# Fewer weight tiles decoded beside attention, a reordered drain and one PSUM layout in a fused attention and feed-forward kernel

## Chip, core and metric

One core of a Trainium2 chip runs the whole program in one launch. The metric is the device time of one execution in microseconds: 1037.8 us before the change, median of 3 runs (1034.76 to 1038.8).

## What is computed

Three stages follow each other. Attention, over 4 batches, 8 heads, 576 positions, 64 columns a head:

```python
scores = scale * np.matmul(q, k.transpose(0, 1, 3, 2))       # causal mask, softmax -> a
local = np.matmul(a, v)
mem_out = einsum(phi(q), M_prev) / (einsum(phi(q), z_prev) + 1e-06)
x = g * mem_out + (1 - g) * local                            # 2304 tokens x 512
```

A first feed-forward stage with weights of 512 x 2048 and 2048 x 512, and a second of two 512 x 1024, one 1024 x 1024 and one 1024 x 512:

```python
h = x @ w_in;  x = (h * np.tanh(softplus(h))) @ w_out
a = x @ w1;  b = x @ w2;  out = ((a * b) @ w3) @ w_out2
```

The weights of the two feed-forward stages come as 64-bit floating-point numbers, and the kernel turns them into 32-bit numbers itself.

## The kernel before, in words

**Decoding weights.** A tile of weights (128 x 512, 64-bit) is loaded as pairs of words into a buffer `draw`; six DVE instructions (L114 to L127) and one POOL addition (L132) turn it into 32-bit numbers `da`; two more POOL instructions split the result into a rounded part and a remainder (L77 and L80, or L160 and L161 where the result goes back to DRAM). `decode` (L104) emits this for a list of tiles, step by step over the list; `run` (L135) takes the next n jobs of a generator. `decoder` (L98) sets up the buffers: one raw buffer and one `da` beside attention, three raw and two `da` in the first feed-forward stage.

**Attention.** There are 16 pairs of heads, p = 0 to 15, in the loop at L521, which also runs once more (p = 16) to finish the last pair. For a pair: scores into `psA` (`s_blocks` L381, `s_last` L397), maximum by DVE (L374), exponential by ACT (L379), normalisation by DVE and POOL (`normed` L358), transposes of the result through `psF` and copies by ACT (`pt_g` L422), and the product with v and the memory matrix in `psX` and `psF` (`pv` L433). `in_turn` (L69) runs a function so that its PE instructions stand behind the PE instruction traced last; before the change that holds from the first transpose on, in the drain at p = 16 too. The compiler's scheduler arranges everything else by a list in which earlier text has priority.

Beside the pairs the kernel decodes weights: at p = 2 to 11 one job each (L559) of a chain of two generators. The first, `lq0`, has the eight tiles of the first quarter of the first feed-forward stage, four of w_in and four of w_out. The second, `pre` (`predecode` L180), has sixteen tiles of the second stage's weights that are decoded early and put back into DRAM.

**First feed-forward stage.** It runs over 4 quarters g of the 2048 hidden columns and 6 chunks n of 384 tokens: 24 units (g, n). `emit_h` (L459) computes h of a unit into four PSUM banks, 48 matmuls of 384 columns, then tanh, arctan and sine by ACT and the product with h by DVE (L493). `split_y` (L496) splits the result y, and `emit_x2` (L593) multiplies it by w_out, again 48 matmuls, and adds into x2 in SBUF (L608, L610). PE runs h of a unit, then x2 of the unit before. Meanwhile the next quarter's eight tiles and the jobs of `pre` are decoded (L691 to L697). In the last quarter w3 and w_out2 are multiplied together (`fold` L615), between h and x2 of each unit.

h and y of unit (0, 0) are made at p = 16, after `pt_g` of group 5 (L553).

**Second feed-forward stage.** `emit_ab` (L739) makes two products a and b for 512 tokens and 128 columns at a time, and `emit_out` (L758) multiplies their product by the folded weights; five of these steps are between the two.

**PSUM before.** Eight banks. In attention: `psA`, two tiles of two banks; X and F, two banks each. After attention that pool is closed and another is opened with three banks A, three X and two F (L578 to L580). h takes A, A, F, F (in the last quarter A, A, A, X; in unit (0, 1) F, X, F, X), x2 takes X, a and b take A, A or A, F in turn, the output of a chunk X, X, X, F.

Of the kernel before, what the change touches and what calls it, by code (L numbers as in the profile page):

```python
# [21 lines left out]
def fused_kernel(ctx: ExitStack, tc, q, k, v, M_prev, z_prev, beta, w_in, w_out, w1, w2, w3, w_out2, out):  # L22
# [19 lines left out]
    sk = ExitStack()  # L42
    pool = [sk.enter_context(tc.tile_pool(name="ps0", bufs=1, space=PSUM))]
    banks = {"X": 2, "F": 2}

    def bank(tag):
        return pool[0].tile([128, 512], F32, tag=tag, name="ps" + tag, bufs=banks[tag])

    def psA():
        return pool[0].tile([128, 2, 512], F32, tag="A", name="psA", bufs=2)  # L50
# [10 lines left out]
    tail = [None]  # L61

# [6 lines left out]
    def in_turn(fn, *args):  # L69

        if tail[0] is None:
            return fn(*args)
        with tc.issue_after(tail[0]):
            return fn(*args)
# [23 lines left out]
    def decoder(stack, raw, n, w=WN):  # L98
        dec.update(pool=stack.enter_context(tc.tile_pool(name="dec", bufs=1)), raw=raw, n=n, w=w)
# [355 lines left out]
    HT = ("AAFF", "AAAX")  # L455
    HU = {(0, 1): "FXFX"}
    gt = {}

    def emit_h(u, beside=iter(())):  # L459
# [7 lines left out]
        for m in range(KQ):  # L467
            if u == (0, 0):
                if m % 2 == 0:
                    two = psA()  # L470
                o = two[:, m % 2, 0:CH]
            else:
                o = bank(HU.get(u, HT[g == NQ - 1])[m])[:, 0:CH]
            ms = slice(128 * m, 128 * m + 128)
            for kk in range(KD):
                mm(o, t[:, 0, kk, ms], x[:, 0, kk, cs], kk == 0, False)
                mm(o, t[:, 0, kk, ms], x[:, 1, kk, cs], False, False)
                mm(o, t[:, 1, kk, ms], x[:, 0, kk, cs], False, kk == KD - 1)
            hp.append(o)
            if m == 1:  # L480
                steps(beside, 1)
# [38 lines left out]
    background = chain(lq0, pre)  # L520
    for p in range(NPAIR + 1):  # L521

        now, old, new = p < NPAIR, p > 0, p + 1 < NPAIR
        if old:
            ensure_x((p - 1) // (2 * NP))
        if not now:
            ek.close()
            wps[0] = wk.enter_context(tc.tile_pool(name="wp", bufs=1, side="right"))
        if p + 2 < NPAIR:
            load_pair(p + 2)  # L530
            load_v(p + 2)
        if now:
            in_turn(s_blocks, p, (3,))
        if old:
            in_turn(pt_g, p - 1, 4)
            in_turn(pt_g, p - 1, 2)
# [11 lines left out]
        if not now:  # L548
            run(lq0, 100)
        if old:  # L550
            in_turn(pt_g, p - 1, 5)
            if not now:
                split = split_y((0, 0), emit_h((0, 0)))  # L553
            in_turn(pt_g, p - 1, 6)
# [4 lines left out]
        if 2 <= p < 12:  # L559
            run(background, 1)  # L560
# [4 lines left out]
        if old:  # L565
            in_turn(pv, p - 1)
        if now:
            in_turn(pt_g, p, 1)
# [6 lines left out]
        if now:  # L575
            normed(p, [(4, None)])
    at.close()
    sk.close()  # L578
    pool[0] = ctx.enter_context(tc.tile_pool(name="ps", bufs=1, space=PSUM))
    banks.update(A=3, X=3)  # L580
# [12 lines left out]
    def emit_x2(u, beside):  # L593
# [4 lines left out]
        for m in range(KD):  # L598
            o = psX()[:, 0:CH]
# [77 lines left out]
    for u in [(g, n) for g in range(NQ) for n in range(NCH)]:  # L677
        g, n = u
        last = g == NQ - 1
        if u not in gt:  # L680
# [4 lines left out]
            y = emit_h(u, folding if last and n > 0 else iter(()))  # L685
# [5 lines left out]
        with tc.issue_after(split):  # L691
            if u == (0, 0):
                run(pre, 2)
            if n == 0:
                run(pre, 2)
            elif not last:
                run(nextq if n < 4 else chain(islice(nextq, 1), islice(pre, 1)), 2)  # L697
        if last and n == 0:
# [41 lines left out]
    def emit_ab(k):  # L740
# [3 lines left out]
        pb, pa = (bank(t)[:, 0:n] for t in ("AA", "AF")[m % 2])  # L744
# [13 lines left out]
    def emit_out(k):  # L758
# [4 lines left out]
        if m == 0:  # L763
            outs[c] = [bank(tag) for tag in "XXXF"[0:n // 128]]
# [63 lines left out]
```

## Time and profile before

| | us |
|---|---|
| median of 3 runs | 1037.8 |
| profiled execution | 1035.9 |
| its span (first to last instruction) | 1034.1 |
| PE busy | 979.9 (95%) |
| DVE busy | 602.9 (58%) |
| ACT busy | 506.9 (49%) |
| POOL busy | 336.2 (33%) |

The profiled execution is a single one; its time is that of the span and what lies around it. Matmuls are pipelined, so a busy PE need not be PE at its fastest. Attention with its drain takes about the first 290 us, the first feed-forward stage runs to about 730 us, and the second to the end.

### The profile page before, as it was taken

The page shows a single profiled execution, that of the slowest core. Times are in us where ns is not written, and L with a number is a line of the kernel's source. Part 1 is how long each engine was busy: PE and PEld are TensorE (multiplying, and loading weights), DVE is VectorE, ACT ScalarE, POOL GpSimd, SP SyncE. Part 2 cuts the span into 40 slices and gives each one's busy share as a digit, 9 for nine tenths or more (in the row PEclk, how much of TensorE's full clock was granted, in tenths as well). Part 3 has the DMA queues.
Part 4 walks back from the last instruction along what each step waited for, and adds up shares of the span by engine and source line. Part 5 has one row for each costly group of instructions (what it writes and reads, how often), then busy time and mean ns, then how long its engine had stood idle before and what let it go on. Part 6 is the DMA issues. An engine that isn't in the chain of part 4 may idle for free.

```text
span 1034.1 us, 15144 instructions
## 1 busy us (share of the span) xinstructions
PE 979.9 (95%) x5584; PEld 830.1 (80%) x5584; DVE 602.9 (58%) x1364; ACT 506.9 (49%) x1016; POOL 336.2 (33%) x345
## 2 busy tenths in 40 slices
PE   5888888999899999999999999999989999999998
PEld 3445455565699999999999999999768888888897
DVE  4888988675377666757575676668973121121111
ACT  4676767888646565565656545443323121221212
POOL 6676666552155334352524221112550000000000
PEclk8998999999999999999999999999999999999999
DMA  7343434320143133112312356222410010100101
GB/s 157 93 114 93 96 93 122 91 52 14 61 143 102 46 117 106 59 61 103 123 41 82 137 193 226 91 78 82 152 41 1 1 41 1 41 1 1 41 1 61
DMA packets 93626, 81.73 MB, mean 79 GB/s; under 512 B 68720, under 2 KB 72816, under 8 KB 93552
## 3 DMA queue, kind: packets, MB, share of 16 engines
q1 hardware_dynamic: 92224, 80.44, 25.2%
q8 instruction: 44, 0.72, 0.3%
q10 hardware_dynamic: 1328, 0.33, 0.2%
q14 instruction: 30, 0.25, 0.1%
HBM read 65.54 MB, written 15.20 MB: 78 GB/s over the span
## 4 chain that ended last, share of the span: by engine, by line
PE 73%; DVE 13%; ACT 7%; POOL 2%; issue 2%; DMA 2%; SPq 0%; ACTq 0%; DVEq 0%; POOLq 0%
PE psX L64 30%; PE psA L64 24%; PE psF L64 17%; ACT s L379 3%; DVE s L374 2%; DVE s L369 2%; PE psF L67 1%; DVE da L118 1%; DVE phie L333 1%; ACT pt L431 1%; POOL s L369 1%; DVE da L114 1%; DVE xt L80 1%; DVE draw L127 1%; PE psF L634 1%
## 5 line engine op out<-in xcount | busy, mean ns | idle before, releaser
L132 POOL TENSOR_TENSOR da<-da,draw 128x512 f32<-128x512 f32 x72 | 104.8, 1464 | 333.6 <-DVE draw L127 253.3
L64 PE MATMUL psX<-gh,wqt 128*128 128x384 f32 x768 | 196.1, 335 | 0.0
L64 PEld LDWEIGHTS psX<-gh,wqt 128*128 128x128 f32 x768 | 138.8, 188 | 1.0 <-DVE y L493 0.3
L64 PE MATMUL psX<-gl,wqt 128*128 128x384 f32 x384 | 128.2, 335 | 0.0
L64 PE MATMUL psA<-xt,wqt 128*128 128x384 f32 x648 | 118.9, 335 | 0.0
L64 PEld LDWEIGHTS psA<-xt,wqt 128*128 128x128 f32 x648 | 112.8, 188 | 0.7 <-DVE s L369 0.2
L379 ACT ACTIVATE s<-s,acc 128x512 f32<-128x512 f32 (+2 forms) x144 | 83.7, 587 | 19.1 <-DVE acc L374 18.4
L67 PEld LDWEIGHTS psF<-ident,s 128*128 128x128 f32 x400 | 44.7, 144 | 55.2 <-ACT pt L431 13.3
L67 PE MATMUL psF<-ident,s 128*128 128x128 f32 x400 | 67.1, 294 | 19.8 <-DVE xt L80 8.0
L64 PE MATMUL psA<-x2h,w12t 128*128 128x512 f32 (+1 forms) x288 | 80.7, 355 | 4.2 <-POOL w12t L77 3.6
L64 PE MATMUL psX<-wft,room 128*128 128x512 f32 x336 | 82.6, 390 | 0.0
L431 ACT COPY pt<-psF 128x512 f32<-128x512 f32 (+1 forms) x112 | 56.9, 538 | 44.8 <-PE psF L67 42.2
L64 PE MATMUL psF<-xt,wqt 128*128 128x384 f32 x408 | 75.2, 339 | 2.8 <-DVE xt L80 2.8
L753 ACT COPY bs<-psA 128x512 f32<-128x512 f32 (+1 forms) x40 | 21.8, 545 | 114.2 <-PE psA L64 106.2
L64 PEld LDWEIGHTS psF<-xt,wqt 128*128 128x128 f32 x408 | 72.4, 191 | 2.9 <-DVE xt L80 2.9
L64 PEld LDWEIGHTS psX<-wft,room 128*128 128x128 f32 x336 | 62.6, 188 | 12.7
L64 PEld LDWEIGHTS psX<-gl,wqt 128*128 128x128 f32 x384 | 72.1, 188 | 0.3
L610 DVE TENSOR_TENSOR x<-x,psX 128x384 f32<-128x384 f32 x72 | 39.6, 549 | 53.7 <-PE psX L64 53.5
L374 DVE CUSTOM_DVE_ANT_0 s<-psA,mask 128x512 f32<-128x512 f32 (+2 forms) x144 | 62.7, 477 | 9.2 <-PE psA L64 9.2
L64 PE MATMUL psA<-x2s,w12t 128*128 128x512 f32 x288 | 67.9, 389 | 0.0
L501 ACT CAST gh<-y 128x768 fp32r<-128x768 f32 x48 | 40.1, 837 | 55.5 <-PE psX L64 53.4
L755 ACT CAST room<-bs 128x512 fp32r<-128x512 f32 (+1 forms) x40 | 23.1, 578 | 84.9 <-DVE bs L754 84.7
(123 smaller groups left out, 1896.2 us busy)
## 6 DMA issues: line engine op xcount, KB each, us to landing
draw<-in_moe_w_dram SPq DMA_DIRECT2D x32, 512.0 KB, 3.7
draw<-in_moe_w_out_dram SPq DMA_DIRECT2D x24, 512.0 KB, 3.8
draw<-in_moe_w_in_dram SPq DMA_DIRECT2D x16, 512.0 KB, 4.0
out_dram<-ob SPq DMA_DIRECT2D x18, 256.0 KB, 2.0
raw<-in_q_dram SPq DMA_DIRECT2D x32, 128.0 KB, 3.2
raw<-in_v_dram SPq DMA_DIRECT2D x32, 128.0 KB, 2.7
o_dram<-draw SPq DMA_DIRECT2D x8, 512.0 KB, 2.8
w_dram<-draw SPq DMA_DIRECT2D x8, 512.0 KB, 2.8
```

The source lines that it names most:

```text
L64: tail[0] = nc.tensor.matmul(o, lhsT=l, rhs=r, start=start, stop=stop).ins
L67: tail[0] = nc.tensor.transpose(o, src, ident).ins
L80: return (eng or nc.vector).tensor_tensor(out=dst, in0=src, in1=f(hi), op=ALU.subtract)
L132: nc.gpsimd.tensor_tensor(out=a, in0=a, in1=lw.bitcast(F32), op=ALU.add)
L369: (nc.gpsimd if x in ON_POOL else nc.vector).tensor_scalar(out=s, in0=s, scalar1=d["sum"][:, x:x + 1], scalar2=og[:, x:x + 1], op0=ALU.mul ...
L374: nc.vector.tensor_tensor_reduce(out=s, in0=o, in1=m, op0=ALU.add, op1=ALU.min, scale=-scale, scalar=init, accum_out=a,)
L379: nc.scalar.activation(out=s, in_=s, func=AF.Exp, scale=-1.0, bias=a, accum_out=r)
L431: nc.scalar.copy(out=t[:, 0:n], in_=o[:, 0:n])
L501: nc.scalar.copy(out=gh, in_=y[i])
L610: r = nc.vector.tensor_tensor(out=d, in0=d, in1=o, op=ALU.add)
L753: nc.scalar.copy(out=bs, in_=pb)
L755: nc.scalar.copy(out=t[:, 0, 0:n], in_=bs)
```

## The change

- Beside the pairs only four jobs of `lq0` are decoded, w_in's four tiles, at p = 3, 6, 9 and 12. w_out's four are decoded at p = 16, two at a time, with a decoder of its own (two raw buffers, two `da`) in the space that attention's early pool has given back.
- The tiles of `pre` come later: none beside pairs, two in unit (0, 0) instead of four, one more each in (1, 0), (1, 2), (2, 0) and (2, 2).
- At p = 16, h of (0, 0) with its y stands first, before the transposes of the last pair; h of (0, 1) follows `pv` of the last pair.
- `in_turn` orders PE only for pairs 1 to 15, and not in pair 0 and the drain.
- PSUM keeps one layout throughout: two `psA` tiles of two banks, two banks X, two F. h takes the two `psA` tiles; x2 takes X and F in turn in quarters 0 to 2 and X alone in the last; a and b take the halves of one `psA` tile; the output of a chunk takes X, F, X, F.

```diff
-    banks = {"X": 2, "F": 2}
+    ps = ctx.enter_context(tc.tile_pool(name="ps", bufs=1, space=PSUM))
...
     def in_turn(fn, *args):
 
-        if tail[0] is None:
+        if not ordered[0]:
             return fn(*args)
...
         for m in range(KQ):
-            if u == (0, 0):
-                if m % 2 == 0:
-                    two = psA()
-                o = two[:, m % 2, 0:CH]
-            else:
-                o = bank(HU.get(u, HT[g == NQ - 1])[m])[:, 0:CH]
+            if m % 2 == 0:
+                two = psA()
+            o = two[:, m % 2, 0:CH]
...
+        ordered[0] = 1 <= p < NPAIR
...
             wps[0] = wk.enter_context(tc.tile_pool(name="wp", bufs=1, side="right"))
+            lk = ExitStack()
+            decoder(lk, 2, 2, side="right")
...
             in_turn(s_blocks, p, (3,))
+        else:
+            split = split_y((0, 0), emit_h((0, 0)))
...
-        if not now:
-            run(lq0, 100)
         if old:
+            if not now:
+                run(lq0, 2)
+                run(lq0, 2)
             in_turn(pt_g, p - 1, 5)
-            if not now:
-                split = split_y((0, 0), emit_h((0, 0)))
             in_turn(pt_g, p - 1, 6)
...
-        if 2 <= p < 12:
-            run(background, 1)
+        if p in (3, 6, 9, 12):
+            run(lq0, 1)
...
             in_turn(pv, p - 1)
+        if not now:
+            early = {(0, 1): emit_h((0, 1))}
...
-            o = psX()[:, 0:CH]
+            o = bank("X" if g == NQ - 1 else "XF"[m % 2])[:, 0:CH]
...
-            y = emit_h(u, folding if last and n > 0 else iter(()))
+            y = early.pop(u) if u in early else emit_h(u, folding if last and n > 0 else iter(()))
...
-            if u == (0, 0):
-                run(pre, 2)
-            if n == 0:
+            if n == 0 and not last:
                 run(pre, 2)
             elif not last:
                 run(nextq if n < 4 else chain(islice(nextq, 1), islice(pre, 1)), 2)
+            if g in (1, 2) and n in (0, 2):
+                run(pre, 1)
...
-        pb, pa = (bank(t)[:, 0:n] for t in ("AA", "AF")[m % 2])
+        pair = psA()
+        pb, pa = pair[:, 0, 0:n], pair[:, 1, 0:n]
...
-            outs[c] = [bank(tag) for tag in "XXXF"[0:n // 128]]
+            outs[c] = [bank(tag) for tag in "XFXF"[0:n // 128]]
```

## Rows read from the trace of the kernel before

**Rows 1.** Page, busy tenths in 40 slices of the span.
```profile
PE   5888888999899999999999999999989999999998
...
DVE  4888988675377666757575676668973121121111
```

**Rows 2.** Windows by stage: start:end, length, busy us (and count) per engine, PEclk, DMA, GB/s.
```profile
27.18:166.18 139.00, 116.34 (x818) 69.29 (x817) 120.18 (x338) 95.22 (x272) 93.41 (x103) 0.95 0.39 98
166.18:196.80 30.62, 27.61 (x205) 16.66 (x204) 24.02 (x76) 23.41 (x67) 18.52 (x22) 0.98 0.43 118
196.80:252.48 55.68, 52.52 (x409) 32.83 (x408) 37.15 (x136) 46.96 (x136) 25.77 (x31) 1.00 0.20 45
252.48:293.41 40.93, 35.78 (x243) 28.66 (x243) 17.89 (x52) 23.48 (x53) 8.88 (x10) 0.96 0.11 39
...
300.00:400.00 100.00, 100.00 (x578) 100.00 (x578) 69.61 (x140) 58.14 (x78) 43.56 (x40) 1.00 0.27 94
```

**Rows 3.** Groups by form, 0 to 235 us, DVE steps of decode: count | busy, mean ns.
```profile
L118 DVE TENSOR_SCALAR da<-da 128x512 int32<-128x512 int32 x10 | 8.0, 797 | 0.2
...
L121 DVE SCALAR_TENSOR_TENSOR da<-draw,da 128x512 int32<-128x512 int32 x10 | 7.1, 710 | 0.0
...
L127 DVE SCALAR_TENSOR_TENSOR draw<-draw 128x512 f32<-128x512 uint32 x10 | 7.0, 697 | 0.0
...
L125 DVE TENSOR_SCALAR draw<-da 128x512 int32<-128x512 int32 x10 | 6.1, 612 | 0.1
...
L114 DVE TENSOR_SCALAR da<-draw 128x512 int32<-128x512 int32 x10 | 5.5, 551 | 8.0 <-POOL wqt L80 7.7 <-DMA draw<-in_moe_w_out_dram 0.3
...
L116 DVE TENSOR_SCALAR da<-da 128x512 f32<-128x512 f32 x10 | 5.0, 503 | 0.2
```

**Rows 4.** Timeline of PE, first matmuls of pairs 1 and 2: start, length.
```profile
27.18 1.17 PE L64 MATMUL psA<-kt,qt 64*128 64x512 f32 x4
...
45.25 1.22 PE L64 MATMUL psA<-kt,qt 64*128 64x512 f32 x2
```

**Rows 5.** Timeline of PE, the drain.
```profile
261.70 2.70 PE L64 MATMUL psA<-xt,wqt 128*128 128x384 f32 x14
...
279.84 0.34 PE L64 MATMUL psF<-phi,mr 128*64 128x64 f32 x4 [1.79 <-ACT pt L431]
...
283.55 3.78 PE L64 MATMUL psF<-xt,wqt 128*128 128x384 f32 x12 [2.79 <-DVE xt L80]
287.17 2.24 PE L64 MATMUL psX<-xt,wqt 128*128 128x384 f32 x12
...
293.41 0.51 PE L64 MATMUL psX<-gh,wqt 128*128 128x384 f32 x2
```

**Rows 6.** Page DMA issue; timelines of SP, DVE and POOL in the drain.
```profile
draw<-in_moe_w_out_dram SPq DMA_DIRECT2D x24, 512.0 KB, 3.8
...
259.82 1.30 SPq L110 DMA_DIRECT2D draw<-in_moe_w_out_dram  x3
...
278.58 1.95 DVE L493 TENSOR_TENSOR y<-y,psA 128x384 f32<-128x384 f32 x4 [12.81 <-ACT y L491]
...
287.87 2.80 POOL L132 TENSOR_TENSOR da<-da,draw 128x512 f32<-128x512 f32 x2 [23.68 <-PE psF L64]
...
291.83 2.54 POOL L161 TENSOR_TENSOR draw<-da,draw 128x512 fp32r<-128x512 f32 x2
```

**Rows 7.** Timelines of DVE and PE, one unit in the middle.
```profile
403.98 0.79 DVE L114 TENSOR_SCALAR da<-draw 128x512 int32<-128x512 int32 x2
...
407.90 1.29 DVE L127 SCALAR_TENSOR_TENSOR draw<-draw 128x512 f32<-128x512 uint32 x2
...
414.62 1.02 DVE L493 TENSOR_TENSOR y<-y,psA 128x384 f32<-128x384 f32 x2 [1.89 <-ACT y L491]
...
418.21 4.32 PE L64 MATMUL psA<-xt,wqt 128*128 128x384 f32 x24
```

**Rows 8.** Timeline of DVE, last quarter.
```profile
711.91 2.25 DVE L80 TENSOR_TENSOR gl<-y,gh 128x768 fp32r<-128x768 f32 x2
```

More of the change, by code (lines that the diff above doesn't have):

```diff
@@ L41, in fused_kernel @@
     dram = ctx.enter_context(tc.tile_pool(name="dram", bufs=1, space=bass.MemoryType.DRAM))
-    sk = ExitStack()
-    pool = [sk.enter_context(tc.tile_pool(name="ps0", bufs=1, space=PSUM))]
-    banks = {"X": 2, "F": 2}
+    ps = ctx.enter_context(tc.tile_pool(name="ps", bufs=1, space=PSUM))
     def bank(tag):
-        return pool[0].tile([128, 512], F32, tag=tag, name="ps" + tag, bufs=banks[tag])
+        return ps.tile([128, 512], F32, tag=tag, name="ps" + tag, bufs=2)
     def psA():
-        return pool[0].tile([128, 2, 512], F32, tag="A", name="psA", bufs=2)
+        return ps.tile([128, 2, 512], F32, tag="A", name="psA", bufs=2)
     def psX():
@@ L61, in fused_kernel @@
     tail = [None]
+    ordered = [False]
     def mm(o, l, r, start, stop):
@@ L96, in fused_kernel, with decoder @@
     dec = {}
-    def decoder(stack, raw, n, w=WN):
-        dec.update(pool=stack.enter_context(tc.tile_pool(name="dec", bufs=1)), raw=raw, n=n, w=w)
+    def decoder(stack, raw, n, w=WN, side="left"):
+        dec.update(pool=stack.enter_context(tc.tile_pool(name="dec", bufs=1, side=side)), raw=raw, n=n, w=w)
     def dec_tile(tag):
@@ L453, in pv @@
             sub(x[:, 1], o[:, 0:q1 - q0], x[:, 0])
-    HT = ("AAFF", "AAAX")
-    HU = {(0, 1): "FXFX"}
     gt = {}
@@ L519, in fused_kernel @@
     pre = predecode()
-    background = chain(lq0, pre)
     for p in range(NPAIR + 1):
         now, old, new = p < NPAIR, p > 0, p + 1 < NPAIR
+        ordered[0] = 1 <= p < NPAIR
         if old:
@@ L576, in fused_kernel @@
             normed(p, [(4, None)])
+    lk.close()
     at.close()
-    sk.close()
-    pool[0] = ctx.enter_context(tc.tile_pool(name="ps", bufs=1, space=PSUM))
-    banks.update(A=3, X=3)
     w2q[0] = ctx.enter_context(tc.tile_pool(name="w2q", bufs=1))
```

## Prediction, made before the change was run

> **What bounds the kernel now.** I read the page's slices first, then busy time by stage, then the timeline of each engine where two stages meet. The slices show three regimes [rows 1]: in the first seven DVE is as busy as PE, then PE is full and DVE mostly at five to seven tenths, and in the last ten DVE is almost idle. So work taken off DVE is worth something in the first quarter only, and DVE work that arrives in the middle is hidden, unless PE has to wait for its result.
>
> By stage [rows 2]: the eight pairs 1 to 8 last 139.00 us, 17.4 each, and DVE is busy for 120.18 of them; pairs 9 and 10 take 30.62, 15.3 each; pairs 11 to 14, with no decoding left, take 55.68, 13.92 each, PE busy 52.52 and DVE 37.15. PE does the same work in each pair. With decoding DVE sets the period, without it PE does. From the start of pair 15 to the first x2 matmul (the drain) it is 40.93 us with PE busy for 35.78. In the feed-forward units PE is busy 100.00 of 100.
>
> **The change, part by part.**
>
> *Six tiles leave the pairs.* The six DVE steps of one tile last 0.55 + 0.50 + 0.80 + 0.71 + 0.61 + 0.70 = 3.87 us [rows 3]. What a tile costs on the path comes out of the periods: pairs 1 to 10 took 139.00 + 30.62 = 169.62 us, ten times 13.92 is 139.2, so ten tiles cost 30.4, or 3.04 each. The last one, alone in pairs 9 and 10, cost 30.62 - 27.84 = 2.78, so distance between tiles makes them little cheaper. Four tiles are left, three pairs apart. At 3.04 each six tiles bring 18.2 us. The bounds: pair 1 took 45.25 - 27.18 = 18.07 [rows 4], 4.15 over an empty pair; if each of the four left cost that, the gain is 30.4 - 16.6 = 13.8. An empty pair leaves DVE 13.92 - 9.29 = 4.6 us of idle time, more than a tile's 3.87; if the four fall wholly into it, the gain is 30.4. I take 18.2, since it is the mean of ten tiles and 2.78 is the nearest single case. The two POOL copies and their loads go with the tile; the loads stand on SP's queue between those of the pairs and nobody is seen waiting for SP there, so that is nothing more.
>
> *The drain.* Before, h of unit (0,0) fills PE from 261.70, but then PE stands 1.79 us for a copy of ACT and 2.79 us for DVE, and the twelve matmuls that follow take 3.78 us where the next twelve take 2.24, some of them at the lower of the two clock levels, 1.2 GHz, after the idle time [rows 5]; the drain's mean granted clock is 0.96 [rows 2]. Idle time 40.93 - 35.78 = 5.15 and the slow matmuls 1.54: 6.7 us could be had. The new order gives h the psA tiles, emits it ahead of the transposes, and lets h of (0,1) start when the product with y frees a psA tile (at 280.5 in the trace [rows 6]), not when pv of pair 15 has given back its bank. PE's own work would then end at 293.41 - 6.7 = 286.7.
>
> Against that, x2 of (0,0) now needs four tiles of w_out which are loaded and decoded here. Two raw buffers make it two rounds. The loads can start when the pairs' tiles on that side are given back, about 259.8, where the trace issues three loads into freed space; a load lands in 3.8 us [rows 6]. DVE needs 5.2 us for two tiles when undisturbed (403.98 to 409.19 [rows 7]) and up to 2 x 3.87 = 7.7 as beside the pairs; POOL needs 6.5 us for two (287.87 to 294.37), and gives the raw buffers back after the first 2.8 [rows 6]. Round one: 263.6, 268.8 to 271.3, raw buffers free at 271.6 to 274.1. Round two: landed at 275.4 to 277.9, DVE done at 280.6 to 285.6, or 287.5 with the 1.95 us product in between; POOL done at 287.1 to 294.0. So x2 of (0,0) starts between 287 and 294 instead of 293.4. I take 290.4, the middle: 3 us gained, from 6.7 gained to 2 lost (a late tile and once more the 1.54 us of the lower clock). On SP the four loads go ahead of the three seen at 259.82, whose tiles nobody needs before the last quarter; on POOL the 13 us of the four tiles stand behind the last scaling steps and ahead of those tiles. On DVE the product, the last two subtractions of pv and the split of y queue behind decode steps, at most one step each, under 1 us. The cover of the decode is h, transposes and pv; behind it there is only h of (0,2), which waits for the product of (0,1).
>
> A row bears on which end it is: the step at L118 has a mean of 0.80 us beside the pairs [rows 3], about twice the 0.4 that a step of its kind takes in the units (0.79 for two [rows 7]). So a DVE step stretches where POOL works. The Trainium skill, "SBUF — State Buffer", section "Who interferes with whom", says that DVE instructions in a two-port mode and GpSimd take one shared pair of ports as an exclusive lock, and the other blocks fully; rows agree as far as they go. By that rule the two rounds overlap at the slow rate, and x2 of (0,0) would start at the late end, near 294.
>
> *Tiles moved into the units.* Four more are decoded in (1,0), (1,2), (2,0) and (2,2), four fewer ahead of that (two of the pairs, two of unit (0,0)). DVE is busy 69.6 of 100 us there [rows 2], 11.6 per unit of 16.6 us (96 of the 578 matmuls that take 100 us); six more steps, half of the 5.2 us of two, make 14.2. They fit, and cost nothing as long as the product is not queued behind them; the cover is PE's own 16.6. If it is gone the price is at most 2.6 us less the 2.6 of slack below, nothing again. Upper bound with waits on POOL: 1 us each, 4 in all.
>
> *PSUM.* h of a unit now takes two tiles of two banks, each given back as a whole, where it had three single A banks and two F. In a steady unit the product that frees the first pair ends at 414.62 + 1.02 = 415.64, and PE begins the next h at 418.21 [rows 7]: 2.6 us of slack, so zero. x2 has four banks for three quarters, more than before. In the last quarter it has two instead of three, and its third block must wait until the first is added. PE needs some 2.1 us per block (2.24 for twelve matmuls with the last one's tail [rows 5]); DVE once has 2.25 us of other work next to such an add [rows 8], and the add itself takes 0.5 like a product (1.02 for two [rows 7]): 2.25 + 0.5 - 2.1 = 0.7 late. Twelve blocks could meet that (two in each of six units): 0 to 8 us, and I take 1, since the window has room for most. The last stage's matmuls keep two products in flight as now: nothing. Pair 0 loses its written order: PE waits there for ACT and DVE anyway, so nothing, 2 us either way.
>
> **Sum.** -18.2 - 3 + 1 = -20.2. The profiled execution is 1035.9 us (span 1034.1), so 1015.7; the median of the three runs, 1037.8, is 1.9 above it, so **1017.6**.
>
> **Rivals.**
> 1. *w_out late.* The decode ends at 294 and PE pays the lower clock again: drain +2 instead of -3, 1022.6. For: two rounds through two raw buffers, POOL slow. Against: DVE stood idle for 12.81 us in that very stretch [rows 6]. 0.16.
> 2. *Half a gain.* The early pairs are slow for another reason: granted clock 0.95 in pairs 1 to 8 against 1.00 in 11 to 14 [rows 2], and if the clock stays there half of the 18.2 goes: 1026.7. Against: the last tile, at 0.98, costs almost as much. If decode steps are merely moved ahead as a lump, it looks the same. 0.12.
> 3. *The four are free,* swallowed by DVE's idle time: 12.2 better, 1005.4. Against: ten tiles had that idle time too and cost 3 us each. 0.08.
> 4. *Slower, by PSUM.* A two-bank tile is held until its second product; if the units' DVE order puts decode steps ahead of it, PE waits once in every unit. It decides when the product ends more than 2.6 us later; for 1043 it takes 1043 - 1017.6 = 25.4 over 22 units, 1.2 us each, a product 3.8 us late, which is most of a two-tile decode (5.2) queued ahead. Against: DVE now runs the products ahead of the decode steps of the next unit. 0.04. The Trainium skill, "Perfetto Trace Analysis", section "Optimization Strategy", takes equal gaps that repeat on the engine that should be saturated as a sign that PSUM is short for the next tile; the trace has none in the units (PE busy 100.00 of 100 [rows 2]), and by that rule this rival would show as one gap per unit ahead of psA.
>
> **How the numbers follow.** Forecast 0.60. Its own range is 1010 to 1029 (pairs 13.8 to 22, the drain 6.7 gained to 2 lost, last quarter 0 to 4), rivals 1 and 2 lie inside it. Left out are rival 3, rival 4 and the tails, so 1009 to 1030. A measurement of this kernel can tell some 0.5%, 5.2 us, from no change: faster means below 1032.6. All but rival 4, a part of rival 2 and mishaps are: 0.91 faster, 0.05 the same, 0.04 slower.
>
> **What would show it.** Pairs without a tile at 13.9 to 14.5 us from pair 1 on, and four longer ones near 17; pair 15 starting at about 234 instead of 252.5; from there to the first x2 matmul about 38 us; PE busy at 100 of 100 in the units with no gap ahead of psA; gaps ahead of psX, at most 1 us in all, in the last quarter. It is wrong if empty pairs stay above 15 us, if PE waits for POOL's w_out tiles by more than 5 us, or if psA gaps recur.

## The result, and the profile after

Beside the kernel before on the same chip the median fell from 1036.41 us (4 runs, 1034.76 to 1038.8) to **1025.53 us** (4 runs, 1023.99 to 1026.82): a ratio of 0.9893, 95% interval 0.9864 to 0.9921. The forecast was 1017.6 with a range of 1009 to 1030, so the sign and the range held and the gain was a little over half of what the sum promised. The profiled execution took 1023.99 us, its span 1022.2 (before: 1035.9 and 1034.1).

The slices of the page of the changed kernel, to lay beside [rows 1]:

```profile
PE   5889999999899999999999999999979999999998
...
DVE  4787667667695759885987576567973121121111
```

DVE has come down to six to eight tenths in most of the first quarter and has gone up in the middle, under a full PE. The one slice in which PE does less than before is slice 30, where the second stage begins: 7 instead of 8.

Busy time by stage of the changed kernel (columns as in [rows 2]: pairs 1 to 8, 9 and 10, 11 to 14, the drain, and a stretch of the units):

```profile
25.25:151.53 126.28, 111.64 (x818) 68.50 (x817) 95.86 (x307) 95.26 (x272) 79.30 (x89) 0.96 0.36 86
151.53:180.74 29.21, 26.09 (x205) 16.43 (x204) 20.74 (x70) 23.84 (x69) 14.54 (x18) 1.00 0.38 86
180.74:236.41 55.67, 52.52 (x409) 32.82 (x408) 37.17 (x136) 46.96 (x136) 25.76 (x31) 1.00 0.19 43
236.41:276.25 39.84, 35.53 (x243) 27.85 (x243) 27.20 (x63) 23.13 (x52) 17.60 (x16) 1.00 0.21 75
300.00:400.00 100.00, 100.00 (x579) 100.00 (x578) 71.03 (x135) 57.03 (x78) 42.55 (x39) 1.00 0.28 94
```

Pairs 1 to 8 went from 139.00 to 126.28 us, pairs 9 and 10 from 30.62 to 29.21, the empty pairs stayed at 55.67, the drain went from 40.93 to 39.84, and the units are full as before. Yet the stretch from h of unit (3,0) to the last matmul became longer. This is that stretch in the kernel before:

```profile
567.97:1030.53 462.56, 457.12 (x2273) 398.80 (x2272) 205.52 (x347) 142.16 (x236) 60.16 (x46) 1.00 0.19 65
```

and in the changed kernel:

```profile
551.91:1018.63 466.72, 458.48 (x2273) 398.29 (x2272) 204.72 (x347) 141.10 (x236) 57.32 (x46) 1.00 0.19 66
```

So 4.2 us of the gain were given back after unit (3,0), 2.8 of them as idle time of PE (8.24 against 5.44 us). From the first matmuls of each stage the whole account is (us, change against before, and the forecast's term):

| stage | measured | forecast |
|---|---|---|
| start and pair 0 (first matmul of pair 1: 27.18 to 25.25) | -1.9 | 0 |
| pairs 1 to 14 (225.30 to 211.16) | -14.1 | -18.2 |
| drain (40.93 to 39.84) | -1.1 | -3 |
| first x2 to h of (3,0) (274.56 to 275.66) | +1.1 | 0 |
| last quarter and second stage (462.56 to 466.72) | +4.2 | +1 |
| sum | -11.9 | -20.2 |

The drain and the units together last 315.49 us before and 315.50 after: the new order there brought nothing by the time of unit (3,0).

The decode steps were not where the code has them. The timeline of DVE of the changed kernel, first step of each of the four tiles:

```profile
29.87 0.94 DVE L113 TENSOR_SCALAR da<-draw 128x512 int32<-128x512 int32 x1 [0.45 <-DMA draw<-in_moe_w_in_dram]
...
48.10 0.78 DVE L113 TENSOR_SCALAR da<-draw 128x512 int32<-128x512 int32 x1
...
62.30 0.43 DVE L113 TENSOR_SCALAR da<-draw 128x512 int32<-128x512 int32 x1 [2.48 <-POOL wqt L79]
...
78.53 0.43 DVE L113 TENSOR_SCALAR da<-draw 128x512 int32<-128x512 int32 x1 [2.42 <-POOL wqt L79]
```

The loop issues them in pairs 3, 6, 9 and 12; the instruction order that the program was given has them in pairs 1 to 4 (which start at 25.25, 44.15, 61.01 and 77.30), 1.2 to 4.6 us into each, ahead of most of the pair's row maxima.

The drain, timeline of PE of the changed kernel, to lay beside [rows 5]:

```profile
246.19 2.65 PE L63 MATMUL psA<-xt,wqt 128*128 128x384 f32 x12
...
262.54 0.33 PE L66 MATMUL psF<-ident,s 128*128 128x128 f32 x1 [1.67 <-ACT pt L430]
...
267.82 8.59 PE L63 MATMUL psA<-xt,wqt 128*128 128x384 f32 x48 [2.65 <-DVE y L487]
276.25 0.51 PE L63 MATMUL psX<-gh,wqt 128*128 128x384 f32 x2
```

PE still stands twice, 1.67 and 2.65 us against 1.79 and 2.79 before. The second wait is now for the gate product. The DVE timeline of the same stage says why it was late:

```profile
264.42 1.40 DVE L124 TENSOR_SCALAR draw<-da 128x512 int32<-128x512 int32 x1
265.86 0.98 DVE L126 SCALAR_TENSOR_TENSOR draw<-draw 128x512 f32<-128x512 uint32 x1
266.76 1.94 DVE L487 TENSOR_TENSOR y<-y,psA 128x384 f32<-128x384 f32 x4
```

ACT's last sine, the product's input, ended at 264.64; the product ran at 266.76, behind the end of the second two w_out tiles' decode. The tiles themselves were not late. The POOL timeline:

```profile
263.92 1.62 POOL L131 TENSOR_TENSOR da<-da,draw 128x512 f32<-128x512 f32 x1 [3.88 <-issue]
...
270.85 1.88 POOL L79 TENSOR_TENSOR wqt<-da,wqt 128x512 fp32r<-128x512 f32 x1
```

It was done at 272.73, 3.5 us ahead of the first x2 matmul.

Waits of PE from h of (3,0) to the end, changed kernel (us in total, times, longest). `w12t` are the decoded tiles of w1 and w2, `wft` and `w3l` belong to the fold:

```profile
PE psA L63 <- DVE bs L752: 4.6, 3, 3.0
PE psA L63 <- POOL w12t L76: 2.1, 3, 1.5
PE psX L63 <- DVE x L607: 1.1, 1, 1.1
PE psX L63 <- DVE wft L79: 0.3, 1, 0.3
PE psA L63 <- POOL w12t L79: 0.2, 1, 0.2
```

and in the kernel before:

```profile
PE psA L64 <- POOL w12t L77: 3.6, 3, 1.5
PE psF L64 <- DVE w3l L80: 1.2, 1, 1.2
PE psA L64 <- ACT bs L753: 0.7, 1, 0.7
```

A wait of 4.6 us for DVE's product of the second stage (bs at L752), which was not there before.

### The profile page after: what moved, and what is told of

Same layout as the page of the kernel before. It is cut to its first block, busy times and chain, and to the rows that moved or that the text cites. A ratio compares the mean times of both kernels' runs of the same rounds, so it can differ in the third digit from the quotient of the medians.

```text
span 1022.2 us, 15101 instructions
## 1 busy us (share of the span) xinstructions
PE 974.3 (95%) x5584; PEld 827.7 (81%) x5584; DVE 615.3 (60%) x1364; ACT 502.7 (49%) x1016; POOL 339.6 (33%) x345
## 4 chain that ended last, share of the span: by engine, by line
PE 69%; DVE 14%; ACT 9%; DMA 3%; POOL 3%; issue 2%; SPq 0%; POOLq 0%; ACTq 0%; DVEq 0%
PE psA L63 35%; PE psX L63 17%; PE psF L63 14%; ACT s L378 4%; DVE s L373 2%; PE psF L66 2%; DVE da L120 1%; DVE draw L126 1%; DVE da L117 1%; ACT pt L430 1%; DVE da L113 1%; DVE s L368 1%; DVE phie L332 1%; DVE draw L124 1%; DVE da L115 1%
## 5 line engine op out<-in xcount | busy, mean ns | idle before, releaser
L63 PE MATMUL psA<-xt,wqt 128*128 128x384 f32 x1152 | 207.5, 335 | 2.9 <-DVE y L487 2.6
L63 PEld LDWEIGHTS psA<-xt,wqt 128*128 128x128 f32 x1152 | 200.0, 188 | 5.1 <-DVE y L487 3.8
L63 PE MATMUL psX<-gh,wqt 128*128 128x384 f32 x480 | 122.3, 335 | 1.1 <-DVE x L607 1.1
L752 DVE TENSOR_TENSOR bs<-bs,psA 128x512 f32<-128x512 f32 (+1 forms) x40 | 25.3, 634 | 160.0 <-ACT bs L751 160.0
L378 ACT ACTIVATE s<-s,acc 128x512 f32<-128x512 f32 (+2 forms) x144 | 83.6, 586 | 12.6 <-DVE acc L373 11.5
L63 PEld LDWEIGHTS psX<-gh,wqt 128*128 128x128 f32 x480 | 86.9, 188 | 2.3 <-DVE x L607 1.4
L63 PEld LDWEIGHTS psA<-x2h,w12t 128*128 128x128 f32 x384 | 68.3, 189 | 20.8 <-DVE bs L752 5.0
L63 PEld LDWEIGHTS psA<-x2s,w12t 128*128 128x128 f32 x384 | 72.1, 188 | 14.9
L63 PE MATMUL psX<-gl,wqt 128*128 128x384 f32 x240 | 80.3, 335 | 0.0
L63 PE MATMUL psF<-gh,wqt 128*128 128x384 f32 x288 | 73.1, 334 | 0.0
L487 DVE TENSOR_TENSOR y<-y,psA 128x384 f32<-128x384 f32 x96 | 48.6, 548 | 33.5 <-ACT y L485 33.5
L63 PE MATMUL psA<-room,w12t 128*128 128x512 f32 (+1 forms) x192 | 68.0, 354 | 0.0
```

Of the source, the lines that this page charges most:

```text
L63: tail[0] = nc.tensor.matmul(o, lhsT=l, rhs=r, start=start, stop=stop).ins
L378: nc.scalar.activation(out=s, in_=s, func=AF.Exp, scale=-1.0, bias=a, accum_out=r)
L487: nc.vector.tensor_tensor(out=y[i][:, j], in0=y[i][:, j], in1=hp[2 * i + j], op=ALU.mult)
L752: nc.vector.tensor_tensor(out=bs, in0=bs, in1=pa, op=ALU.mult)
```

## The experiments

The theories at the start. **A:** the two-bank psA tiles cost the end of the kernel about 5 us, because the second stage's first bank is no longer given back when ACT has copied it, but with DVE's product. Rival: the fold is merely later, and POOL's w12t sets the end whatever the banks. **B:** ten tiles cost less than 3.04 us each, since part of the long pairs is the start's; rival: the price was right and something else in the pairs went wrong. Every row below counts from first matmuls; "tail" is h of (3,0) to the last matmul. Each row is one trace, and each ratio is to the kernel before on the same chip; medians of different sections need not come from one chip.

| kernel | pair 15 at | pairs 1-14 | drain | first x2 to (3,0) | tail | end |
|---|---|---|---|---|---|---|
| before | 252.48 | 225.3 | 40.9 | 274.6 | 462.6 | 1030.5 |
| changed | 236.41 | 211.2 | 39.8 | 275.7 | 466.7 | 1018.6 |
| e1 | 253.62 | 226.9 | 36.7 | 279.4 | 468.2 | 1037.9 |
| e2 | 241.18 | 215.8 | 42.0 | 275.2 | 464.5 | 1023.0 |
| e3 | 227.60 | 203.8 | 39.3 | 275.6 | 469.2 | 1011.7 |
| e4 | 238.43 | 211.3 | 41.3 | 275.5 | 466.6 | 1021.9 |
| e5 | 236.52 | 210.4 | 37.1 | 279.8 | 468.7 | 1022.1 |
| e6 | 239.67 | 214.5 | 49.9 | 278.5 | 462.3 | 1030.3 |
| e7 | 246.88 | 220.7 | 38.6 | 275.4 | 470.2 | 1031.0 |
| e8 | 233.18 | 207.1 | 39.8 | 275.5 | 467.1 | 1015.6 |
| e9 | 233.49 | 207.7 | 41.2 | 275.5 | 468.7 | 1018.9 |
| e10 | 233.58 | 207.5 | 41.4 | 275.5 | 469.3 | 1019.8 |
| e11 | 232.87 | 207.2 | 41.4 | 275.5 | 465.0 | 1014.8 |
| e12 | 233.01 | 207.3 | 37.2 | 280.9 | 464.8 | 1016.0 |

### The PSUM layout alone (e1)

The kernel before with only the layout of the change (the main lines of the edit; the single pool and the banks of x2 and of the output go with them):

```diff
-                o = bank(HU.get(u, HT[g == NQ - 1])[m])[:, 0:CH]
+            if m % 2 == 0:
+                two = psA()
+            o = two[:, m % 2, 0:CH]
...
-        pb, pa = (bank(t)[:, 0:n] for t in ("AA", "AF")[m % 2])
+        pair = psA()
+        pb, pa = pair[:, 0, 0:n], pair[:, 1, 0:n]
```

> The kernel before with the new PSUM layout alone (two two-bank tiles for h and for the products a and b, x2 in X and F, or X alone in the last quarter); decoding and drain as before. Theory A, the two-bank tiles cost at the start of the second stage, where the trace after the change shows three PE waits of 0.43, 1.08 and 3.05 us for the product that frees a tile: about 4 us slower than before, near 1040, with such waits ahead of psA between 730 and 780 us. Theory B, the start of the second stage is set by the decoding of the last eight tiles on DVE and POOL, and a PE wait for a tile only takes the place of a wait for weights: within 1 us of before, near 1036.

Measured: 1043.62 us median of 9 runs, ratio 1.0062 (1.0039 to 1.0084). The tail became 468.2 against 462.6, with the same 4.6 us of waits for DVE's product as in the changed kernel. So the layout by itself costs 5.7 us there. The drain became 4.3 us shorter: h of (0,1) no longer waits for a bank of pv. That was lost again three units later: the way to (3,0) is 4.8 us longer, 3.0 of it one wait (timeline of PE of this kernel, as in the rows above):

```profile
335.13 2.29 PE L62 MATMUL psA<-xt,wqt 128*128 128x384 f32 x6 [3.04 <-DVE y L488]
```

### Single banks instead of two-bank tiles (e2)

The changed kernel, with each psA tile made of two single banks, given back one by one:

```diff
-        return ps.tile([128, 2, 512], F32, tag="A", name="psA", bufs=2)
+        return Two([ps.tile([128, 512], F32, tag="A", name="psA", bufs=4) for _ in range(2)])
```

> The changed kernel with the two-bank tile split into two tiles of one bank each, so that each bank is given back by itself; same banks, same order of the text. Theory A: the waits for the product go and the time falls by 3 to 4.5 us, to about 1021.5. Theory B: waits for POOL's weight tiles take their place, 1025 within 1 us.

Measured: 1027.76 us, 4 runs, ratio 0.9895 (0.987 to 0.992), not to be told from the changed kernel. The tail came down from 466.7 to 464.5, and PE's waits in it changed so:

```profile
PE psA L70 <- POOL w12t L83: 3.8, 3, 2.4
PE psA L70 <- DVE bs L759: 1.2, 1, 1.2
PE psA L70 <- ACT bs L758: 1.1, 1, 1.1
PE psX L70 <- DVE x L614: 0.7, 1, 0.7
```

Both theories had a part: waits for the product fell from 4.6 to 1.2, and those for POOL rose from 2.3 to 3.8. What was won was lost ahead of it: the empty pairs take 14.38 us instead of 13.97, pair 15 starts 4.8 us later, and the drain is 2.2 us longer.

### No tile beside the pairs (e3)

```diff
+    for c in range(KD):
+        next(lq0)
+        for i in range(2):
+            nc.gpsimd.memset(f(wts[0][:, i, c]), 0.01)
-        if p in (3, 6, 9, 12):
-            run(lq0, 1)
```

> The changed kernel without any decoding beside the pairs: w_in's four tiles of the first quarter are not decoded but filled with a constant by POOL at the start, so four loads and decodes are left out. Theory C, a tile beside the pairs costs 3.04 us as in the trace before: pair 15 starts 12 us earlier, near 224 instead of 236.4. Theory D, what is left above 13.97 us per pair after the change, 15.6 us over pairs 1 to 14, is all the tiles' and they cost 3.9 each: near 221. Theory E, the early pairs are slow by themselves (start, low clock): pairs 1 to 4 stay at 15 us or more without any tile, and pair 15 starts later than 228.

Measured: 1017.51 us, pair 15 at 227.60, so the four tiles cost 8.8 us, 2.2 each. But the fourteen pairs last 203.8 us where fourteen of 13.97 are 195.6, and 6.4 of the difference are one pair, the first, without any tile. Busy time in that pair, columns as before:

```profile
23.77:44.11 20.34, 18.33 (x109) 11.57 (x108) 14.55 (x42) 13.04 (x36) 12.96 (x15) 0.75 0.33 74
```

PE is busy for 18.33 of 20.34 us at a granted clock of 0.75, so it worked a good part of the pair at 1.2 GHz. I took this for the price of the start, paid in any kernel, and concluded that a tile in pair 1 is free. That reading fell with e8, where pair 1 without a tile took 15.00 us.

### Pair 0 in its written order (e4)

```diff
-        ordered[0] = 1 <= p < NPAIR
+        ordered[0] = p < NPAIR
```

> The changed kernel with the written PE order also in pair 0, as it was before; the drain stays free. If the 1.9 us by which pair 1 starts earlier after the change (25.25 against 27.18 us) come from the freed order of pair 0: pair 1 starts near 27 again. If they are worth something at the end, pair 15 starts 2 us later than 236.4; the rival is that pair 1 gives them back (it lasted 18.89 instead of 18.07 us), then pair 15 starts within 1 us of 236.4.

Measured: 1027.2 us, one run; pair 1 starts at 27.10 instead of 25.25 and pair 15 at 238.43 instead of 236.41. By this one run the freed order of pair 0 is worth 2.0 us. The other traces make it less sure: with the freed order pair 1 starts at 25.2 to 26.2 (ten kernels, e3 left out), with the written one at 26.7 to 27.2 (before, e1, e4), so 0.5 to 2.0 us.

### The product ahead of the second round of decode (e5)

The second two tiles' DVE steps are held behind the first unit's product:

```diff
                 run(lq0, 2)
-                run(lq0, 2)
+                with tc.issue_after(prod[0]):
+                    run(lq0, 2)
```

> The changed kernel with the second round of w_out's decode steps on VectorE put behind the first unit's gate product, which stood behind them (the product ran at 266.76 us while its inputs were there at 264.64, and h(0,1) began at 267.82). Theory: the product is what the drain lost. h(0,1) begins 2 us earlier against the start of the drain, the first x2 matmul comes about 2 us earlier (274 instead of 276.25), the end about 2 us earlier (1022 profiled). Rival: w_out's last tile then lands later and the first x2 matmul waits for it, x2 unmoved within 0.7 us, the end with it. In both, the 14 pairs before stay at 211.2 us.

Measured: 1027.52 us, 4 runs, ratio 0.9876 (0.9848 to 0.9905). The first half of the theory held: the wait is gone, the drain is 37.1 us, 2.7 shorter, and the first x2 matmul comes at 273.66. The second half fell, and not to the rival either. A later unit's product stood behind decode steps instead:

```profile
317.64 2.75 PE L64 MATMUL psA<-xt,wqt 128*128 128x384 f32 x10 [2.21 <-DVE y L488]
```

2.2 us of waiting, and behind it a granted clock of 0.83 from 318 to 328 us. The way to (3,0) is 4.1 us longer, the end 3.5 later than in the changed kernel.

### The old layout after attention (e6)

```diff
     at.close()
+    sk.close()
+    pool[0] = ctx.enter_context(tc.tile_pool(name="ps", bufs=1, space=PSUM))
+    banks.update(A=3, X=3)
```

with h, x2 and the second stage on the banks that they had before.

> The changed kernel with the PSUM layout of before from the end of attention on (three A, three X and two F banks), all else as changed. Theory A (the two-bank tiles cost the last quarter and the second stage): attention and drain as in the changed kernel (pair 15 at 236.4, first x2 at 276.3), the waits of TensorE for VectorE's product in the second stage fall from 4.6 us to under 1, and the end comes 4 us earlier: about 1020 us profiled, ratio to the kernel before 0.984. Rival B (the tail is lost to the fold being later, whatever the banks): the end moves by 1 us or less (about 1024), what the product gives back is taken by waits for POOL's w12t.

Measured: 1032.77 us, 6 runs, ratio 0.9925 (0.9896 to 0.9955). In the tail theory A is borne out: 462.3 us, as before, and no wait for DVE's product at all:

```profile
PE psA L65 <- POOL w12t L78: 3.5, 3, 1.5
PE psF L65 <- DVE w3l L81: 1.2, 1, 1.2
PE psA L65 <- ACT bs L758: 0.7, 1, 0.7
```

So the layout costs 4.4 us there. What I had not foreseen is the switch of the pools itself, right behind h of (0,1), which now runs in the drain:

```profile
289.56 0.98 PE L65 MATMUL psX<-gh,wqt 128*128 128x384 f32 x2 [7.03 <-POOL draw L162]
```

The first x2 tile of the new pool waited 7.03 us, the drain took 49.9. The POOL instruction named there uses no PSUM. The last use of the old pool's tiles is the product with y of (0,1), on the timeline of DVE:

```profile
287.46 1.95 DVE L492 TENSOR_TENSOR y<-y,psA 128x384 f32<-128x384 f32 x4 [0.61 <-ACT y L490]
```

It ended at 289.41, and PE began at 289.56. So the wait was most likely for this product; no run separates it from the pool's other users. With h of (0,1) in the drain, the one layout spares this.

### All eight tiles beside pairs (e7)

```diff
-        if p in (3, 6, 9, 12):
+        if 2 <= p < 10:
             run(lq0, 1)
```

and none in the drain.

> The changed kernel with all eight tiles (w_in's four and w_out's four) decoded beside pairs, one per pair from pair 2 on, and none in the drain. If a tile beside a pair costs 2.2 us, pair 15 starts about 8.8 us later than in the changed kernel (245 instead of 236.4), and the drain (39.8 us there) is shorter by what w_out's decode costs it: by 2 to 3 us (to about 37) if the product queued behind decode steps is the cost, by under 1 us if TensorE's own work bounds it anyway. Theory: 37, so that the first x2 matmul comes near 282 and the end about 6 us later than the changed kernel. Rival: the tiles are cheaper spread out, 1 us each, and the end is within 2 us.

Measured: 1036.42 us, one run. Pair 15 starts at 246.88, 10.5 us later, 0.9 of it because pair 1 starts later; pairs 1 to 14 take 220.7 us instead of 211.2, so the four added tiles cost 9.5 us, 2.4 each. Without decode the drain is 38.6 us, 1.3 shorter. The theory's 37 was missed by 1.6, its direction held. Its end, 6 us later, was missed too: 1031.0 is 12.4 us later, 3.5 of it in the tail (470.2). Eight tiles: 220.7 - 195.6 = 25.1 over empty pairs, 3.1 each.

### The four tiles held where the code has them (e8, e9)

```diff
         if p in (3, 6, 9, 12):
-            run(lq0, 1)
+            with tc.issue_after(last[0]):
+                run(lq0, 1)
```

where last[0] is the pair's last row maximum issued so far.

> The changed kernel with the VectorE steps of the four tiles held in pairs 3, 6, 9 and 12, where the code writes them, instead of pairs 1 to 4 where they ran. Theory: pair 1 lasts until 44.1 us even without a tile, so a tile in it is free, and the other three cost 2.2 to 3 each; held in four later pairs all four cost, pair 15 starts 2 to 3 us later than 236.4 (238.5 to 239.5). Rival: a tile costs the same wherever it is, pair 15 at 236.4 within 0.5 us. Third: spread out they hide better, pair 15 earlier by 2 us or more.

Measured: 1020.94 us, one run. The third case came true: pair 15 at 233.18, 3.2 us earlier, and pairs 1 to 14 in 207.1 us, 18.2 less than before. That is the forecast's term to the tenth, with the tiles where the forecast had them. What the fourteen pairs take over fourteen empty ones is 207.1 - 195.6 = 11.5 us, 2.9 for each of the four tiles; in the changed kernel 15.6, or 3.9. Not all of that is the tiles': pairs 3 and 4 of e8 together take 30.3 us and pairs 12 and 13 30.4, against 27.9 for two empty ones, so 2.4 a tile. The match to the tenth is thus in part luck. And pair 1, without a tile as in e3, takes 15.00 us:

```profile
26.11:41.11 15.00, 14.23 (x103) 8.38 (x102) 10.82 (x38) 11.71 (x34) 11.36 (x14) 0.94 0.49 114
```

at a granted clock of 0.94 where e3 had 0.75. So e3's 20.34 us are no fixed price of the start; why that run had the lower clock there stays open, and e3 does not measure a tile.

The same kernel timed:

> The kernel of e8_tiles_pinned again, timed. Theory C (where the four tiles run is what the forecast missed: they ran in pairs 1 to 4, at 3.6 us each over 13.97 us pairs, and held in pairs 3, 6, 9 and 12 they cost 2.6): 1020 to 1022 us median, ratio to the kernel before 0.983 to 0.986, pair 15 at 233.2 within 0.7 us. Rival: that one look was a lucky one, 1025 as the changed kernel.

Measured: 1025.03 us, 4 runs (1023.58 to 1025.85), ratio 0.987 (0.9839 to 0.9902), which can't be told from the changed kernel. Pair 15 at 233.49 confirms the pairs; the time does not confirm e8. The two traces of one kernel differ in two places, each behind a wait of PE. Busy time in e8 in 5 us behind the wait for the first product, and in 5 us behind the longest wait in the second stage:

```profile
265.00:270.00 5.00, 5.00 (x31) 5.00 (x30) 3.34 (x5) 3.45 (x5) 4.41 (x3) 1.00 0.00 0
763.59:768.59 5.00, 5.00 (x22) 4.16 (x23) 2.07 (x3) 1.81 (x3) 0.00 (x0) 1.00 0.01 3
```

and in e9:

```profile
265.00:270.00 5.00, 5.00 (x21) 5.00 (x22) 3.67 (x6) 2.90 (x3) 4.74 (x4) 0.72 0.00 0
765.27:770.27 5.00, 5.00 (x15) 3.93 (x16) 2.08 (x3) 1.80 (x3) 0.00 (x0) 0.66 0.01 3
```

31 matmuls against 21, and 22 against 15: in e9 part of these stretches ran at 1.2 GHz. It costs 1.4 us in the drain (41.2 against 39.8) and 1.7 in the tail (468.7 against 467.1). Such a cut is common: the 48 matmuls of h of (0,1) take 8.6 us in the changed kernel and in e8, 9.9 in e9 and 10.1 to 10.2 in e4, e10 and e11. The profiled execution of the changed kernel, the fastest of its four, has 1.00 in both places, so it flatters the changed kernel against e9.

### The same hold, but in pairs 1 to 4 (e10)

```diff
-        if p in (3, 6, 9, 12):
+        if 1 <= p <= 4:
```

with the hold of e8.

> The changed kernel with the VectorE steps of the four tiles held behind the pair's last row maximum as in e8_tiles_pinned, but in pairs 1 to 4. Theory C1 (the early pairs are what is dear: TensorE has its clock cut there while it is held up): pairs 1 to 5 take 83 to 85 us as in the changed kernel (83.6), pair 15 at 236 to 237. Theory C2 (the place within the pair is what counts, steps behind the maxima hold up nothing): a tile costs 2.6 us as in e8_tiles_pinned wherever it is, pairs 1 to 14 take 207 us and pair 15 starts at 233.

Measured: 1025.31 us, 2 runs. Pair 15 at 233.58, pairs 1 to 14 in 207.5 us, pairs 1 to 5 in 80.4 against 83.6: these are C2's numbers, not C1's. Held behind the maxima, the tile of pair 2 starts at 49.85, 7.8 us into the pair, where in the changed kernel it started 3.9 us into it:

```profile
49.85 0.42 DVE L114 TENSOR_SCALAR da<-draw 128x512 int32<-128x512 int32 x1
```

But pair 2 did not get shorter by it: 17.5 us, against 16.9. The lengths by first matmuls show where the hold saves time (us; the number of tiles in brackets):

| kernel | pair 1 | pairs 2 to 5 | pairs 6 to 10 | pairs 11 to 14 |
|---|---|---|---|---|
| changed | 18.9 (1) | 64.7 (3) | 71.9 (0) | 55.7 (0) |
| e10, held early | 16.0 (1) | 64.4 (3) | 71.4 (0) | 55.7 (0) |
| e8, held late | 15.0 (0) | 59.2 (1) | 74.8 (2) | 58.1 (1) |
| e3, no tile | 20.3 (0) | 56.4 (0) | 71.2 (0) | 55.8 (0) |

Of the 3.7 us between the changed kernel and e10, 2.9 are pair 1's. In pairs 2 to 5 a tile costs nearly the same on either side of the maxima: over e3's 56.4 it is 2.8 each in the changed kernel and 2.7 in e10. (e4, e5 and e6, with the tiles not held, have 65.1 to 66.5 there, and 18.2 to 18.9 in pair 1.) In pair 1 of the changed kernel PE waits 2.33 us for a DVE step of the normalisation (L368) that stands behind decode steps, in e10 0.37 us, which fits a tile ahead of the maxima that holds up the chain. Yet e3 has no tile and the longest pair 1, and pairs 0 and 1 together take 35.65 us there, 35.72 in the changed kernel, 33.36 in e10 and 32.57 in e8. So what the hold changes in the first two pairs, beyond the tile itself, is open.

### Single banks for the second stage alone, on e8 (e11)

psA has a pool of its own, opened anew behind the units, when nothing is in it:

```diff
+    sk.close()
+    pool[0] = ctx.enter_context(tc.tile_pool(name="psb", bufs=1, space=PSUM))
     split_x2(0)
...
-        pair = psA()
-        pb, pa = pair[:, 0, 0:n], pair[:, 1, 0:n]
+        pb, pa = (pool[0].tile([128, 512], F32, tag="A", name="psA", bufs=4)[:, 0:n] for _ in range(2))
```

> e8_tiles_pinned with psA in a PSUM pool of its own, which is opened anew after the units as four single banks, for the second stage's products alone. Up to the units' end all is as in e8_tiles_pinned (pair 15 at 233.2, first second-stage matmul at 703.9). Theory A: the waits of TensorE for VectorE's product fall from 4.6 to about 1.2 us as in e2_single_banks, the end comes 2 us earlier than in e8_tiles_pinned (1017 profiled, ratio to the kernel before 0.980 to 0.984). Rival: waits for POOL's w12t take up what the product gives back, the end is unmoved within 0.7 us.

Measured: **1020.58 us**, 4 runs (1018.83 to 1021.45), ratio 0.9825 (0.9798 to 0.9851). Its interval lies below that of the changed kernel (0.9864 to 0.9921), so by their ratios to the kernel before it is faster than the changed kernel. The tail is 465.0, and PE's waits in it:

```profile
PE psA L67 <- POOL w12t L80: 4.0, 3, 2.6
PE psA L67 <- DVE bs L756: 1.2, 1, 1.2
PE psX L67 <- DVE x L612: 1.1, 1, 1.1
```

The product's share fell as theory A said, POOL's rose as the rival said, and the tail is 2 us shorter than in e8 and 3.7 shorter than in e9. Against e9, which ran on the same chip, the median is 4.4 us lower; part of it is that the 3 us wait, behind which e9's clock was cut, is gone.

### Four buffers for the decode in the drain, on e11 (e12)

```diff
-            decoder(lk, 2, 2, side="right")
+            decoder(lk, 4, 4, side="right")
```

> e11_pinned_single_late with four raw and four work buffers instead of two of each for w_out's decode in the drain, so that the second two tiles' steps need not wait for GpSimd to finish the first two (they began 5.5 us after the first two's end there, and the first unit's gate product stood behind them). Theory: the second two's steps follow the first two's at once and are over before the product's inputs come, TensorE's wait of 2.6 us ahead of h(0,1) falls under 0.6 and the clock is not cut behind it (0.66 from 265 to 270 us in e11_pinned_single_late): the first x2 matmul comes 2 to 3.5 us earlier against pair 15's start (38 to 39.5 us after it instead of 41.4), the end 2 to 3 us earlier than in e11_pinned_single_late (1015 to 1017 profiled, ratio to the kernel before 0.979 to 0.981). Rival: as in e5_product_ahead a later unit gives it back, with a product behind decode steps there, and the end is within 0.7 us of e11_pinned_single_late.

Measured: 1022.81 us, 6 runs, ratio 0.9849 (0.9822 to 0.9875). Again the first half held (drain 37.2 us, no wait ahead of h of (0,1)), and then a later unit took all of it back, as the rival said, and by the profile 1 us more: h of (0,2) now waits.

```profile
282.46 1.97 PE L67 MATMUL psA<-xt,wqt 128*128 128x384 f32 x5 [3.79 <-DVE y L491]
```

The DVE timeline ahead of it:

```profile
278.61 1.39 DVE L128 TENSOR_SCALAR draw<-da 128x512 int32<-128x512 int32 x1
280.03 0.98 DVE L130 SCALAR_TENSOR_TENSOR draw<-draw 128x512 f32<-128x512 uint32 x1
280.93 0.55 DVE L610 COPY x<-psX 128x384 f32<-128x384 f32 x1
281.40 1.00 DVE L491 TENSOR_TENSOR y<-y,psA 128x384 f32<-128x384 f32 x2
```

ACT's sine had ended at 276.08; the product stood behind seven more steps of the next tiles.

## Why the prediction was right, and where it was wrong

**The reading of the bound held.** Empty pairs 11 to 14 stay at 13.92 us [rows 2], where PE sets the period, and pairs 1 to 8, with four tiles left in them, fell by 12.7 us. Faster by over 0.5% came out, with 11.9 us by the profile instead of 20.2.

**The six tiles (-18.2 forecast, -14.1 measured): the price was nearly right, the place and the empty pairs were not.** The step "Four tiles are left, three pairs apart" took the place in the code for the place in the instruction stream, where they stood in pairs 1 to 4. The missing 4.1 us are in two places. Pair 1 took 18.9 us, 5.0 over 13.92 instead of the 3.04 of a tile: 1.9 us. And pairs 6 to 10, which have no tile left, took 71.9 us where five times 13.92 is 69.6: 2.3 us; e3 without any tile has 71.2 there. So the period of pairs 11 to 14, which the forecast used for every empty pair, is too short for the earlier ones, and its 3.04 a tile will have held some of that. In pairs 2 to 5 the three tiles cost 9.1 us over four times 13.92, 3.0 each, as forecast. With the tiles held, the fourteen pairs come to -18.2 (e8), -17.6 (e9) and -18.1 (e11). The bound of 13.8 was nearly met, but not by its mechanism, in which every tile costs what pair 1 did; that it bounded the result is luck. The other end of the range has 22 for the pairs, for which the prediction gives no working (its bound was 30.4); its terms add up to 1009 to 1030, not 1010 to 1029.

Rival 2 lost half of the 18.2 us; 4.1 were lost. Its remark that tiles moved ahead as a lump would look the same came true, as the four ran in consecutive pairs. Its cause, early pairs that are slow by themselves, is ruled out by e3 for pairs 2 to 5: 56.4 us without a tile, against 55.7 for four late pairs. For pair 1 it is open: without a tile it took 20.3 us in e3, at a granted clock of 0.75, and 15.0 in e8, at 0.94. Rival 3, free tiles, is ruled out: held late, a tile still cost 2.4 us. My own theory B, a tile at 2.2, rested on e3 as a whole, whose pair 1 is no measure of a tile.

**The drain (-3 forecast, -1.1 measured, 0.0 with the units).** The step that failed is "On DVE the product, the last two subtractions of pv and the split of y queue behind decode steps, at most one step each, under 1 us": the product stood behind the decode for 2.1 us (264.64 to 266.76), and PE waited 2.65. w_out itself was ready 3.5 us ahead of time, so rival 1 fell. But the deeper error is that the forecast booked an earlier first x2 matmul as gain. In e1, e5 and e12 the drain was 36.7 to 37.2 us, and the way from there to (3,0) 279.4 to 280.9 instead of 275.7 in the changed kernel: each time another unit's product stood behind decode steps, and PE waited 3.0, 2.2 and 3.8 us for it. Drain and units together are 315.5 before, 315.5 after, 316.1 to 318.1 in these three.

The forecast weighed a rule on the decode in the drain. A row bears on it: the step at L124 that began at 264.42, while POOL's addition ran (263.92 to 265.54), took 1.40 us, where the three others of its line in the drain took 0.41 or 0.42. The Trainium skill, "SBUF — State Buffer", section "Who interferes with whom", says that a DVE instruction in a two-port mode and GpSimd take the shared ports for a whole instruction, and the other blocks; the trace agrees. It did not decide the end: by it the forecast had the first x2 some 41.5 us into the drain, it came at 39.8, and no matmul of x2 waited for POOL.

**The units (0 forecast, +1.1).** Rival 4 did not come: PE is busy 275.42 of 275.66 us there, with no wait listed. Before it was busy for all of 274.56, so most of the 1.1 us is PE at work for longer. Eight other kernels with these units have 275.2 to 275.6; no run was made on the cause.

**PSUM in the last quarter and the second stage (+1 forecast, +4.2).** The +1 for x2's blocks was one wait of 1.1 us. The step that failed is "The last stage's matmuls keep two products in flight as now: nothing." Two products are in flight as before, but a bank was given back when ACT had copied it, and the pair of banks is given back with DVE's product: 4.6 us of waits that the same layout brings to the kernel before (e1), and that fall to 1.2 with single banks (e2, e11) and to none with the old layout (e6). About 2.2 us come back with single banks (e2), 4.4 with the old layout (e6). What makes the other 2.2 is open; with single banks PE's waits sum to 6.8 us, with the old layout to 5.4. The size also moves: nine traces with the two-bank tiles have a tail of 466.6 to 470.2 us, so the changed kernel's 466.7 is near the low end.

**Pair 0 (0, 2 either way; -1.9).** e4 points to the freed order, for 0.5 to 2.0 us. The cover named ("PE waits there for ACT and DVE anyway") did not change: PE's idle time in pair 0 is 5.3 us before (18.60 less 13.28 busy) and 5.3 after (16.82 less 11.47). What fell is its busy time, and why is open.

## What to carry to other kernels

Where a scheduler orders the instructions, price a moved step at the place where the stream has it, and look there after the change: four tiles written in pairs 3, 6, 9 and 12 ran in pairs 1 to 4, and holding them behind the row maxima took 3.5 to 4.1 us off pairs 1 to 14 in five kernels (e8 to e12), though what the hold changes in pair 1 is not settled. Take the price of an empty stretch from the place where the steps are taken away: empty pairs 6 to 10 were 2.3 us longer than five late ones. In all three kernels in which the drain lost a wait, a wait came back in a later unit, where DVE had decode steps queued ahead of a product; count a gain only at a point behind which nothing can take it back. A tile of two banks is one buffer: what could be given back in halves is held until the last reader is done.

## What was not expected of the hardware

One and the same kernel had its TensorE clock cut behind waits of 2.67 and 3.05 us in one execution (e9: 0.72 and 0.66 over the next 5 us) and not behind waits of 2.62 and 3.05 us in another (e8: 1.00 both times); where it is cut, a wait costs 1.4 to 1.7 us more than itself. The two executions differ by over 3 us with nothing changed, so a single profile does not rank two versions that close. The Trainium skill, "TensorE: Matmul & The Clock Gate", Part 1 on the clock gate, says that the number of slow matmuls at a kernel's start differs between runs of one kernel; these two traces show the same in the middle of a kernel.
